# Splitting the load of V's first weight half in the head, and joining two late loads of the down weights

## The chip, the cores and the metric

The kernel runs on one core of a Trainium2 chip. The metric is the device time of one execution in microseconds (us); lower is better. Three runs of the kernel before took 308.35 to 308.47 us, the median is 308.46 us.

The core has a matrix engine (TensorE, PE in the profile; its weight loads are listed apart as PEld), a vector engine (VectorE, DVE), a scalar engine (ScalarE, ACT), GpSimd (POOL) and a queue processor (SyncE, SP) that issues transfers between the device memory (DRAM) and the core's working memory. Sixteen transfer engines carry them out. Matrix products accumulate in banks of a memory of their own (PSUM).

## The reference

One input x of 2048 rows and 640 columns goes through two branches, and their results are added to x. Only A_x is used as x; B_x has the same shape and is ignored by the reference's sum.

```python
def _A_ref(x, wqkv, wo):            # H = 32 heads of Dh = 20, window W = 256
    qkv = (x @ wqkv).reshape(B, S, 3, H, Dh).transpose(2, 0, 3, 1, 4)
    q, k, v = qkv[0], qkv[1], qkv[2]
    scores = einsum("bhqd,bhkd->bhqk", q, k) * (Dh ** -0.5)
    mask = (idx[:, None] - idx[None, :] >= 0) & (idx[:, None] - idx[None, :] < W)
    p = softmax(where(mask, scores, -1e9))
    o = einsum("bhqk,bhkd->bhqd", p, v)
    return o.transpose(0, 2, 1, 3).reshape(B, S, D) @ wo

def _B_ref(x, w_gate, w_up, w_down):   # F = 1536
    h = sigmoid(x @ w_gate) * (x @ w_up)
    return h @ w_down

xn = layernorm(x)
return x + _A_ref(xn, wqkv, wo) + _B_ref(xn, w_gate, w_up, w_down)
```

All arrays are bfloat16.

## The kernel before

**Tiling.** The 2048 rows are four chunks (c = 0 to 3) of 512 rows, each of four row blocks of 128 (s = 0 to 3). The 640 columns of x are five contraction blocks of 128 (DC = 5, index d), the 1536 hidden columns twelve blocks (FC = 12, index f). The query, key and value weights are one tile `wqkv` of 128 x 5 x 1920; V's part is its last 640 columns, handled as two halves of 320 (HALF). `wg`, `wu` and `wd` hold the gate, up and down weights, `wo` the output weights.

**The order of instructions is the order of the program text.** Nothing is rescheduled: every engine and every queue works through its own instructions in the order in which the code issues them, and an instruction waits until the results and transfers that it needs are there. SP issues nearly all loads and stores, one after the other, so that an issue that waits holds up those behind it.

**The head** (lines 141 to 163, then 671 to 729). SP first issues three row blocks of x (s = 0, 1, 3; `load_rows`), then V's first half with `load_v(0)` (one transfer, all five contraction blocks), then row block 2, V's second half with `load_v(1)`, the q and k weights (`load_wqkv`), and the first halves of block 0 of `wg` and `wu` (lines 162 and 163). The rest of `wg` and `wu` comes later, when other steps have passed; the second half of block 0 of `wu` is issued at line 409, between the first loads of the spread q and k.

TensorE starts with ten dummy products (`warm`, line 202). VectorE and ScalarE normalise the row blocks in the order 0, 1, 3, 2; TensorE transposes each normalised block (`turn_pieces`, tile `pt`; five transposes), and the transposed pieces are copied to `xnT`, contraction blocks 0 to 2 in one copy and 3 to 4 in another. In TensorE's order come: the transposes of row block 0, three dummy products, the transposes of row block 1, V's first half of row blocks 0 and 1 (`v00`, `v10`, five products each, lines 692 and 697), the transposes of row block 3, `v01`, `v30`, `v11`, the transposes of row block 2, and the remaining V products. `project_v` (line 317) runs over d = 0 to 4 and takes `wqkv[:, d, ...]` as the moving operand. Then the q and k projections of chunk 0 follow (`proj_block`, tile `pqk`), whose results go through `st` tiles to DRAM (`sq`, `sk`) and come back spread over the partitions (`spread`, tiles `qT` and `kT`).

**The steady part.** `fill` is a list of pieces of TensorE work (gate and up products `gu...`, projections `qk...` and `v...`, output `out...`), pulled between the steps of the attention so that TensorE always has something to do. Some pieces only issue transfers. Among them, line 743 issues the blocks 0 to 7 of the down weights in three transfers, and the piece "wd" (line 750) the blocks 8 to 11 in four, one block each, behind the q and k work of chunk 1 and ahead of V of chunk 1; the piece "wo" (line 752) then loads the output weights with four transfers, and `g_out` (line 485) loads rows of x and uses `wd` in `down` (line 452). In `down`, f runs from 0 to 11, so blocks 8 to 11 are needed last.

Of the kernel before, what the change touches and what calls it, by code (L numbers as in the profile page):

```python
# [15 lines left out]
DC = D // P  # L16
FC = F // P
# [7 lines left out]
HALF = 320  # L25
# [44 lines left out]
def kernel(  # L70
# [11 lines left out]
    nc = tc.nc  # L82
# [37 lines left out]
    wqkv = const.tile([P, DC, 3 * D], BF16, name="wqkv")  # L120
    wqkv_r = A_wqkv.rearrange("(c p) n -> p c n", p=P)
    wg = [const.tile([P, DC, FS], BF16, name=f"wg{k}") for k in range(F // FS)]
    wu = [const.tile([P, DC, FS], BF16, name=f"wu{k}") for k in range(F // FS)]
    wd = const.tile([P, FC, D], BF16, name="wd")
# [9 lines left out]
    def load_rows(s, queue):  # L134
        queue.dma_start(out=xc[0][:, s, :], in_=xr[:, s, :])  # L135

    def load_v(hf):
        a = 2 * D + hf * HALF
        nc.sync.dma_start(out=wqkv[:, :, a:a + HALF], in_=wqkv_r[:, :, a:a + HALF])

    load_rows(0, nc.sync)
    load_rows(1, nc.sync)
    load_rows(3, nc.sync)
    load_v(0)
    load_rows(2, nc.sync)
    load_v(1)
    load_wqkv(0)
    load_wqkv(1)
# [246 lines left out]
    def g_qk(c, behind={}):  # L395
        for w in "qk":
            for m in range(DC):
                proj_block(w, c, m)
                behind.get((w, m), lambda: None)()
                yield 5 * MM  # L400
        if c:
            spread("q", c, 0, 2)
            spread("k", c, 0, 2)
        else:
            for r in range(2):
                spread("q", c, r, r + 1)
                spread("k", c, r, r + 1)
                if r == 0:
                    load_gu(wu, B_w_up, 0, FS // 2)

    def g_v(c):
        for s in range(SBC):
            new_v(c, s)
            for b in range(2):
                both_v(c, s, b, nc.scalar.copy if b else nc.vector.tensor_copy)
            if s == 1 and c > 1:
                spread_rest(c)
            yield 10 * 136
# [210 lines left out]
    def mix(a, b, first, every=1, rest=True):  # L629

        for k, cost in enumerate(a):
            yield cost
            if k >= first and (k - first) % every == 0:
                yield next(b, 0)
        if rest:
            yield from b
# [94 lines left out]
    fill = Fill()  # L731
# [3 lines left out]
    def later(load, *args):  # L735
        load(*args)
        yield 0
# [9 lines left out]
    fill.add("gu0a", mix(g_gu(0, 0, 6), first, 0), 6 * GU)  # L747
    fill.add("gu0b", mix(g_gu(0, 6, 9), beside, 0), 3 * GU)
    fill.add("qk1", g_qk(1, behind1), 50 * MM)
    fill.add("wd", later(load_wd, ((8, 9), (9, 10), (10, 11), (11, FC))), 0)  # L750
    fill.add("v1", mix(g_v(1), norms2, 2, 1, False), 40 * 136)
    fill.add("wo", later(load_wo), 0)
    fill.add("gu0c", mix(g_gu(0, 9, 12), norms2, 0, 1, False), 3 * GU)
# [112 lines left out]
```

## Time and profile before

| What | us |
|---|---|
| median of three runs | 308.46 |
| the profiled execution | 308.37 |
| its span (first to last instruction) | 306.6 |
| TensorE busy in the span | 302.8 |
| VectorE busy | 192.1 |
| ScalarE busy | 193.1 |
| GpSimd busy | 83.4 |

The granted TensorE clock is full in the whole span. The second part of the page cuts the span into 40 slices; two of its lines show how the transfers are spread. "DMA" is the busy share of the sixteen transfer engines in tenths, "GB/s" what they moved:

```profile
DMA  7998889879029522721052022550000210000301
GB/s 212 348 277 259 282 253 324 227 237 224 9 82 275 149 86 94 227 69 71 18 128 87 25 76 88 175 183 0 3 2 5 68 40 24 2 2 3 88 21 64
```

The transfers are dense in the first quarter of the span, where all weights come in, and thin after it. A slice is 7.7 us long, so the whole head lies in the first two.

In a chain or timeline a line reads: start, duration, engine, line of the code or tile, and how often. In the view of waits it reads: who waited, `<-`, for whom, total time, number of times, longest time. In the view of transfers: destination, `<-`, source, the issuing queue, how often, size, and the time from issue to landing.

### The profile page before, as it was taken

How to read it: one execution, taken by the hardware profiler on the slowest of the kernel's cores; microseconds unless marked ns; L12 is line 12 of the kernel's file. 1: busy time of each engine (PE TensorE's matmuls, PEld its weight loads, DVE VectorE, ACT ScalarE, POOL GpSimd, SP SyncE). 2: the span in 40 equal slices, each digit the busy share in tenths (PEclk: the TensorE clock that was granted, in tenths of full speed). 3: DMA queues.
4: the chain of work that ended last, by engine and by line, in shares of the span. 5: the costliest groups of instructions: out<-in, count | busy, mean ns of one | idle time of the engine just before them, and what ended most of it. 6: DMA issues, size and time to landing. Idle time of an engine off the chain costs nothing.

```text
span 306.6 us, 10171 instructions
## 1 busy us (share of the span) xinstructions
PE 302.8 (99%) x4434; PEld 165.5 (54%) x4434; DVE 192.1 (63%) x391; ACT 193.1 (63%) x183; POOL 83.4 (27%) x189
## 2 busy tenths in 40 slices
PE   8999999999999999999999999999999999999996
PEld 3654444564556654644556644644446665444774
DVE  5778899298984489487643666364483627465523
ACT  6923785977775458867656557768765466778000
POOL 5021234635314123512213132341314132221100
PEclk9999999999999999999999999999999999999999
DMA  7998889879029522721052022550000210000301
GB/s 212 348 277 259 282 253 324 227 237 224 9 82 275 149 86 94 227 69 71 18 128 87 25 76 88 175 183 0 3 2 5 68 40 24 2 2 3 88 21 64
DMA packets 35788, 36.86 MB, mean 120 GB/s; under 512 B 2976, under 2 KB 35488, under 8 KB 35744
## 3 DMA queue, kind: packets, MB, share of 16 engines
q1 hardware_dynamic: 34336, 33.84, 37.0%
q0 software_dynamic: 544, 1.61, 1.7%
q10 hardware_dynamic: 864, 0.77, 0.9%
q8 instruction: 34, 0.56, 0.8%
q14 instruction: 10, 0.08, 0.1%
HBM read 25.59 MB, written 11.44 MB: 121 GB/s over the span
## 4 chain that ended last, share of the span: by engine, by line
PE 97%; DMA 1%; ACT 0%; DVE 0%; SPq 0%; issue 0%
PE pg L431 18%; PE y L454 18%; PE pu L440 17%; PE pqk L283 15%; PE ps L517 9%; PE y L461 7%; PE acc L550 6%; PE pv L341 6%; PE pv L321 1%; DMA xc<-in_A_x_dram 1%; PE pt L236 0%; PE pvh L321 0%; ACT turn L657 0%; PE pwarm L200 0%; DVE turn L230 0%; SPq L135 0%
## 5 line engine op out<-in xcount | busy, mean ns | idle before, releaser
L523 ACT ACTIVATE pT<-ps 128x2048 bf16<-128x2048 f32 x75 | 140.8, 1877 | 55.0 <-PE ps L517 32.5
L506 POOL TENSOR_SCALAR_AFFINE_SELECT pT<-pT 64x256 bf16<-64x256 bf16 (+1 forms) x126 | 67.1, 532 | 179.6 <-ACT pT L523 121.6
L431 PE MATMUL pg<-xnT,wg 128*128 128x512 bf16 x240 | 59.9, 380 | 0.0
L440 PE MATMUL pu<-xnT,wu 128*128 128x512 bf16 x240 | 59.8, 380 | 0.0
L454 PE MATMUL y<-wd,h 128*128 128x320 bf16 (+2 forms) x396 | 56.8, 295 | 0.0
L444 DVE SCALAR_TENSOR_TENSOR h<-th,pu 128x512 bf16<-128x512 f32 x48 | 32.8, 683 | 35.0 <-ACT th L434 19.4
L454 PEld LDWEIGHTS <-h 128*128 128x128 bf16 x396 | 36.8, 98 | 15.9 <-issue 2.3
L534 DVE TENSOR_TENSOR pT<-pT,keep 128x512 bf16<-128x512 bf16 (+2 forms) x81 | 35.8, 449 | 15.0 <-ACT pT L523 14.2
L283 PE MATMUL pqk<-xnT,wqkv 128*128 128x512 bf16 x185 | 43.7, 380 | 0.0
L434 ACT ACTIVATE th<-pg 128x512 f32<-128x512 f32 x48 | 28.6, 595 | 20.2 <-PE pg L431 19.9
L440 PEld LDWEIGHTS <-wu 128*128 128x128 bf16 x240 | 22.2, 98 | 27.3 <-issue 2.2
L431 PEld LDWEIGHTS <-wg 128*128 128x128 bf16 x240 | 21.7, 98 | 26.4 <-issue 2.9
L517 PE MATMUL ps<-qT,kT 20*64 20x320 bf16 (+4 forms) x1440 | 32.0, 260 | 0.0
L561 DVE STREAM_TRANSPOSE t<-acc 128x512 f32<-128x512 f32 x32 | 21.0, 694 | 17.1 <-PE acc L550 17.1
L465 DVE SCALAR_TENSOR_TENSOR rows<-y,rows 128x320 bf16<-128x320 f32 x30 | 14.2, 488 | 25.3 <-PE y L461 20.4
L283 PEld LDWEIGHTS <-wqkv 128*128 128x128 bf16 x185 | 18.5, 103 | 19.7 <-issue 0.8
L517 PEld LDWEIGHTS <-kT 20*64 20x64 bf16 x1440 | 13.5, 103 | 27.4 <-issue 27.4
L461 PE MATMUL y<-wo,oc 128*128 128x320 bf16 (+2 forms) x165 | 24.2, 295 | 0.0
L550 PE MATMUL acc<-pT,v 64*32 64x320 bf16 (+4 forms) x1440 | 20.0, 253 | 0.0
L461 PEld LDWEIGHTS <-oc 128*128 128x128 bf16 x165 | 15.5, 98 | 6.7 <-issue 1.0
L550 PEld LDWEIGHTS <-v 64*32 64x32 bf16 x1440 | 17.0, 92 | 3.4 <-issue 0.9
L341 PE MATMUL pv<-wqkv,xnT 128*64 128x320 bf16 x240 | 17.4, 300 | 0.0
(65 smaller groups left out, 190.4 us busy)
## 6 DMA issues: line engine op xcount, KB each, us to landing
qT<-sq SPq DMA_DIRECT2D x16, 256.0 KB, 4.3
kT<-sk SPq DMA_DIRECT2D x16, 256.0 KB, 4.6
xc<-in_A_x_dram SPq DMA_DIRECT2D x16, 160.0 KB, 4.3
sq<-st SPq DMA_DIRECT2D x20, 128.0 KB, 3.4
sk<-st SPq DMA_DIRECT2D x20, 128.0 KB, 3.1
out_dram<-rows SPq DMA_DIRECT2D x15, 160.0 KB, 1.8
wg<-in_B_w_gate_dram SPq DMA_DIRECT2D x4, 480.0 KB, 7.9
wu<-in_B_w_up_dram SPq DMA_DIRECT2D x4, 480.0 KB, 7.6
```

The lines of the kernel that those rows point to most:

```text
L283: nc.tensor.matmul(ps, lhsT=wt[:, m, :], rhs=xnT[c][:, :, d, :], start=(d == 0), stop=(d == DC - 1))
L341: nc.tensor.matmul(ps[hf * U:(hf + 1) * U, 0:HALF], lhsT=xnT[c][:, s, d, rows], rhs=wqkv[:, d, 2 * D + hf * HALF:2 * D + (hf + 1) * HALF], ...
L431: nc.tensor.matmul(pg, lhsT=part(wg, d, f), rhs=xnT[c][:, :, d, :], start=(d == 0), stop=(d == DC - 1))
L440: nc.tensor.matmul(pu, lhsT=part(wu, d, f), rhs=xnT[c][:, :, d, :], start=(d == 0), stop=(d == DC - 1))
L444: nc.vector.scalar_tensor_tensor(out=h, in0=th, scalar=1.0, in1=pu, op0=ADD, op1=MULT)
L454: nc.tensor.matmul(y[:, 0:cut[1] - cut[0]], lhsT=ht[c, f][:, s * P:(s + 1) * P], rhs=wd[:, f, cut[0]:cut[1]], start=(f == 0), stop=False)
L461: nc.tensor.matmul(y[:, 0:cut[1] - cut[0]], lhsT=oc[c, m][:, s * P:(s + 1) * P], rhs=wo[:, m, cut[0]:cut[1]], start=False, stop=(m == DC - 1))
L506: nc.gpsimd.affine_select(out=part, in_=part, pattern=pattern, compare_op=GE, fill=0.0, base=-1 if sign > 0 else 0, channel_multiplier=sign)
L517: nc.tensor.matmul(ps[side * U:(side + 1) * U, i, col * U:(col + n) * U], lhsT=qk["k", kc, half][32 * i:32 * i + DH, 2 * r + side, kb * U: ...
L523: nc.scalar.activation(out=pt[:, :, 0:used, :], in_=ps[:, :, 0:used * U], func=EXP, scale=SCALE)
L534: nc.vector.tensor_tensor(out=part, in0=part, in1=limit.to_broadcast([P, HG, n * U]), op=MIN)
L550: nc.tensor.matmul(accs[side][32 * i:32 * i + 32, q * U:(q + n) * U], lhsT=vt[sb][rows, b, at:at + 32], rhs=pt[rows, i, col:col + n, :], s ...
```

## The change

V's first half is loaded by two transfers, contraction blocks 0 to 2 and 3 to 4, in the place of one. The second of them stands ahead of row block 2 in SP's order. The late part of the down weights is loaded by three transfers in the place of four: blocks 8, 9, and 10 with 11. The number of transfers in the whole program stays the same. No product, copy or other instruction of an engine is changed.

```diff
-    def load_v(hf):
+    def load_v(hf, lo=0, hi=DC):
         a = 2 * D + hf * HALF
-        nc.sync.dma_start(out=wqkv[:, :, a:a + HALF], in_=wqkv_r[:, :, a:a + HALF])
+        nc.sync.dma_start(out=wqkv[:, lo:hi, a:a + HALF], in_=wqkv_r[:, lo:hi, a:a + HALF])
 
     load_rows(0, nc.sync)
     load_rows(1, nc.sync)
     load_rows(3, nc.sync)
-    load_v(0)
+    load_v(0, 0, 3)
+    load_v(0, 3, DC)
     load_rows(2, nc.sync)
     load_v(1)
     load_wqkv(0)
...
-    fill.add("wd", later(load_wd, ((8, 9), (9, 10), (10, 11), (11, FC))), 0)
+    fill.add("wd", later(load_wd, ((8, 9), (9, 10), (10, FC))), 0)
```

## The prediction

> **What bounds the kernel now.** I read the page first: busy shares and the chain that ended last.
>
> ```profile
> span 306.6 us, 10171 instructions
> PE 302.8 (99%) x4434; PEld 165.5 (54%) x4434; DVE 192.1 (63%) x391; ACT 193.1 (63%) x183; POOL 83.4 (27%) x189
> PE 97%; DMA 1%; ACT 0%; DVE 0%; SPq 0%; issue 0%
> ```
>
> TensorE (PE) makes up 97% of the chain, so a transfer counts only where TensorE stands still for it. Next, who TensorE's matmuls waited for; this is the view's whole answer for the run:
>
> ```profile
> PE pwarm L200 <- PEq L850: 0.8, 1, 0.8
> PE pt L236 <- DVE turn L230: 0.2, 1, 0.2
> ```
>
> No matmul waits for a transfer anywhere. Then the chain in order of time over the head, 3 to 14 us:
>
> ```profile
> 3.51 0.83 ACT turn L657 x2
> ...
> 6.44 0.45 PE pt L236 x5
> 6.89 1.36 PE pv L321 x10
> 8.25 0.30 PE pt L236 x5
> 8.54 1.36 PE pv L321 x10
> 9.90 0.68 PE pvh L321 x5
> ```
>
> The pieces join end to end: row block 1's transposes (`pt`), then the ten V matmuls (`pv`, first the five of `v00`) at 0.136 us each. The timeline has the first `pv` start at 6.73, one step after the fifth transpose began (6.44 + 5 x 0.058). Ahead of 6.44 the weight loads stood 0.53 us until VectorE's norm of row block 1 (L668): the head is set by row block 1, not by V's weights.
>
> The timeline of the SP queue gives the issues:
>
> ```profile
> 2.19 0.43 SPq L139 DMA_DIRECT2D wqkv<-in_A_wqkv_dram  x1
> 2.67 0.52 SPq L135 DMA_DIRECT2D xc<-in_A_x_dram  x1
> 3.23 0.43 SPq L139 DMA_DIRECT2D wqkv<-in_A_wqkv_dram  x1
> ```
>
> and the transfer view, asked one issue at a time, gives the time to landing. These are V's first half, issued at 2.19, and the second half of `wu`'s block 0, issued at 27.13:
>
> ```profile
> wqkv<-in_A_wqkv_dram SPq DMA_DIRECT2D x1, 400.0 KB, 4.3
> wu<-in_B_w_up_dram SPq DMA_DIRECT2D x1, 480.0 KB, 4.2
> ```
>
> So V's first half lands at 2.19 + 4.3 = 6.5, 0.24 us before its first use at 6.73. The `wu` piece lands at 27.13 + 4.2 = 31.33; TensorE needs it at 31.60 (`pu` of f = 3, whose columns begin at 384). That 0.27 us is the thinnest cover that I found behind the head.
>
> **The change, part by part.**
>
> *The wait that splits.* `v00`'s matmuls d = 0 to 2 now wait for the first piece, d = 3 and 4 for the second. The first is issued where the whole was (2.19) and carries 3/5 of the bytes. At best it lands earlier; at worst it keeps 4.3 us: 6.5 against 6.73, no stall and no gain, because row block 1's transposes stand ahead of it in TensorE's order. The second piece is issued one issue later. I take 0.48 us for that, the distance 2.67 - 2.19. With the whole 4.3 us kept it lands at 6.97, and d = 3 starts at 6.73 + 3 x 0.136 = 7.14. Cover left: 0.17 us. Behind the possibly waiting matmul stand all of TensorE's later matmuls; the value is 0 at both bounds. No row shows the cost of one more semaphore wait on a matmul. The nearest are the gaps marked issue, 0.02 to 0.04 us each in the head's chain; I take 0 and keep 0 to 0.04.
>
> *The issue added on SP.* Everything behind it moves 0.48 us later in issue: rows 2, V's second half, q and k weights, the first `wg` and `wu` pieces. Whether the landings move too depends on whether the 16 transfer engines run out of work. By the stage table they moved 51, 236, 325, 246, 159, 161, 244 GB/s in the half microseconds from 1.5 on, some 306 KB by 3.0 us. After the change the SP queue will have issued 491 KB of rows (three of 160 x 1024 bytes) plus 410 KB of V by 3.1 us: some 550 KB still pending, over 1.5 us of work at the later 350 GB/s. So I take 0 for the landings. The other end is the whole 0.48 us, with the same time to landing for each:
>
> - rows 2: 2.67 + 4.3 = 7.0 becomes 7.45. ScalarE takes it up at 7.26 (L657), so 0.19 late; its norm ends at 10.11, then 10.30, and TensorE transposes it at 10.42. Covered.
> - V's second half: 3.23 + 4.8 = 8.03 becomes 8.51; `v01` starts at 8.38. Stall 0.13.
> - q weights: 3.71 + 6.6 = 10.3; first used at 12.74. Covered by 2.4.
> - The `wu` piece at 31.33 hangs on the stream through a chain: the first q store lands late behind some 2 MB of loads, ScalarE's k copies wait for its `st` buffer until 21.94, the last k store follows, then `kT`, which SP waits for, and then the `wu` issue at 27.13. A delay of 0.48 would pass down it: 31.81 against 31.60, a stall of 0.21, which contains the 0.13 if that was already paid.
>
> So the sum over the head lies between 0 and +0.21 (0.25 with the wait's 0.04).
>
> *Transfers counted.* The extra transfer moves no extra bytes: pieces of 640 bytes in both. Its own time on the engines beyond bytes has no row here. From below it is 0; from above, the smallest issue-to-landing time in the head, 2.2 us (row block 1), if none of that ran beside other work. Row blocks 0, 1 and 3 land at 3.1, 3.5 and 4.6, though each took 2.2 to 2.9; most of that time therefore overlaps. The nearest row is the 0.4 us between the first two landings, about what 164 KB needs at 350 GB/s (0.47), so I take 0.
>
> The Trainium skill speaks against this edit: "DMA: Bandwidth & Descriptors", section Rules for kernel authors, says to coalesce small transfers into large ones, and its section on the anatomy of one DMA gives about 2.0 us of fixed cost each (a fit for transfers issued from GpSimd). [...]
>
> *The down weights.* Issues of 160 KB four times become 160, 160 and 320 KB:
>
> ```profile
> 66.80 1.90 SPq L172 DMA_DIRECT2D wd<-in_B_w_down_dram  x4
> 69.01 2.72 SPq L184 DMA_DIRECT2D wo<-wo_i  x4
> 72.13 1.11 SPq L471 DMA_DIRECT2D rows<-in_A_x_dram  x2
> 88.78 0.38 SPq L256 DMA_DIRECT2D turn<-turn  x1
> ```
>
> One issue goes, 1.90 / 4 = 0.48 us on SP; `wo` and `rows` may be issued that much sooner. TensorE's first down matmuls (`y`, L454) start at 81.81. The last piece, issued near 67.8, would land by 75.0 even with the 7.2 us that a 480 KB piece of `wd` took at most. `wo` (69 to 71.7, some 6.9 to landing) is used at 88.14. SP afterwards stands 15.2 us for VectorE's `turn` before 88.78, which takes up any shift. Value 0 both ways, covered by 6.8 us at the least.
>
> SP also waits for older transfers: it stood 0.4 us for a `wd` piece twice ahead of the `rows` loads. That looks like a wait for the transfer eight issues back. If so, one more transfer in the head makes the `wg` and `wu` issues wait for row blocks 1 and 3, landed by 4.6, before those issues (5.8 and later), and the count is level again after `wd`. Value 0.
>
> Sum: 0, with ends -0.06 (one transpose step, if V's landing was hidden in rounding) and +0.25. The profiled execution took 308.37 us: 306.6 of span and 1.77 around it. The median of the runs is 308.46, 0.09 above. I predict 308.45.
>
> **Rivals.**
>
> 1. *V's landing did set the start.* Earlier weights gain what TensorE lost to them. For it: 6.5 against 6.73 is thin. Against: `pt` and `pv` join without a gap, and before 6.44 VectorE was late. If row block 1 also landed sooner because less was queued behind it, the most would be ScalarE's idle time before it, 0.49 us: 307.97. A gain over 0.2% has no place that I can name, as TensorE never stands later.
> 2. *Slower: the late issue reaches the `wu` piece.* Place: `pu` of f = 3 at 31.60. It decides once the stream is more than 0.27 us later at the q stores. At 0.48 us it costs 0.21: 308.67. To pass 0.2% the delay must exceed 0.62 + 0.27 = 0.89 us, nearly two issues; for it only that engines moved just 160 GB/s from 3.5 to 4.5, a stretch that I can't explain and in which the added transfer lies.
> 3. *Slower: the extra transfer's fixed time stands in series.* Everything behind it lands 2.2 us later: V's second half at 10.2 against 8.38 stalls 1.85, and the `wu` piece (33.5 against then 33.45) hardly adds. 308.45 + 1.9 = 310.35. Against: the landings 0.4 us apart. With the skill's 2.0 us in its place this would be 0.2 us less.
> 4. *The split does nothing,* both pieces landing together at 6.5: 308.45, not to be told from the forecast by time.
>
> **How the numbers follow.** A measurement of this kernel tells about 0.2%, 0.62 us, from no change. No change (with rival 4): 0.55. Rival 1: 0.17; what I can price of it stays below 0.62 us, and 0.05 goes there; 0.12 is kept for a gain over the line by something of the head's transfers that the trace of before doesn't show. Rival 2: 0.20, of it 0.03 at its priced 0.21 us and 0.17 where the delay is more than I bounded. Rival 3: 0.08. So faster 0.12, within 0.55 + 0.05 + 0.03 = 0.63, slower 0.17 + 0.08 = 0.25. The likeliest case's own range is 308.2 to 308.7. The range from 307.9 to 309.2 takes in rival 1's bound and a stall of rival 2 up to 0.75 us, and leaves out rival 3 and the far ends.
>
> **What would show it.** In the changed profile: two `wqkv` issues of 240 and 160 KB from 2.19 on and rows 2 issued near 3.15; first `pv` still at 6.73 behind `pt` with no gap; `pvh` and `pqk` starts unmoved within 0.1; `pu` of f = 3 at 31.6. I am wrong if a matmul waits for `wqkv` or `wu`, if `pt` of row block 1 moves from 6.44, or if the steady stage after 45 us takes another length.

## The result: 0.3 to 0.4% slower

The changed kernel took 309.46 us (median of 8 runs, 308.87 to 310.15) against 308.47 us (8 runs, 308.35 to 308.93): ratio 1.0031, interval 1.0022 to 1.0041. Two repetitions in the later comparisons gave 1.0043 (1.0029 to 1.0057) and 1.0033 (1.0023 to 1.0043). The profiled execution took 309.37 us, its span is 307.6 us, 1.0 us over that of the kernel before.

The page of the changed kernel, span, busy shares and the chain by engine:

```profile
span 307.6 us, 10172 instructions
PE 303.1 (99%) x4434; PEld 165.6 (54%) x4434; DVE 192.2 (62%) x391; ACT 193.2 (63%) x183; POOL 83.2 (27%) x189
PE 95%; DMA 3%; SPq 1%; issue 0%; DVE 0%
```

A transfer now has 3% of the chain, and the queue processor 1%. Whom TensorE's matmuls waited for, the view's whole answer (who, `<-`, for whom: total us, times, longest; the first line is the start of the program and stood there before too):

```profile
PE pwarm L201 <- PEq L851: 0.8, 1, 0.8
PE pqk L284 <- DMA wqkv<-in_A_wqkv_dram: 0.6, 1, 0.6
PE pt L237 <- DVE turn L231: 0.2, 1, 0.2
```

and the chain in order of time from 3 to 15 us:

```profile
3.70 0.43 SPq L139
...
4.18 0.53 SPq L129
...
4.75 9.18 DMA wqkv<-in_A_wqkv_dram
...
13.97 1.06 PE pqk L284 x4
```

The loss is whole by 14 us. Matmul by matmul, the shift against the kernel before is 0.13 us at the first transposes, 0.21 at `v01` (8.60 against 8.38) and 0.98 at the second `pqk` (13.97 against 12.99); later it stays there. That second product of q waits for the transfer issued at 4.75: the **k** weights, not q's. The program has this wait in both kernels: the second weight load of q waits for the semaphore of the k transfer, though it reads q's columns alone. In the profile of before it left one line, in the view of the weight loads' waits:

```profile
PEld L283 <- DMA wqkv<-in_A_wqkv_dram: 0.3, 1, 0.3
```

The k weights landed there at 12.95, just as TensorE came to them. With the change they land at 13.93. The timelines of the weight loads have that place, first in the kernel before, then in the changed one (start, duration; in brackets how long the weight loads stood before it, and for whom):

```profile
12.99 1.67 PEld L283 LDWEIGHTS <-wqkv 128*128 128x128 bf16 x9 [0.27 <-DMA wqkv<-in_A_wqkv_dram]
```

```profile
13.97 0.59 PEld L284 LDWEIGHTS <-wqkv 128*128 128x128 bf16 x4 [1.04 <-DMA wqkv<-in_A_wqkv_dram]
```

How the transfers moved. Issues on SP after the change:

```profile
2.18 0.96 SPq L139 DMA_DIRECT2D wqkv<-in_A_wqkv_dram  x2
3.19 0.47 SPq L135 DMA_DIRECT2D xc<-in_A_x_dram  x1
3.70 0.43 SPq L139 DMA_DIRECT2D wqkv<-in_A_wqkv_dram  x1
```

The two pieces took 3.7 and 3.6 us to land (5.9 and 6.3), and row block 2 landed at 6.7: all **earlier** than before (6.5 and 7.0), although the last two were issued 0.5 us later. V's second half, issued at 3.70, landed at 8.6 against 8.0. What lies between is in the stage table. Its last two columns are the busy share of the transfer engines (above 1 where packets overlap) and GB/s; first the kernel before, then the changed one:

```profile
5.00:7.00 2.00, 1.75 (x16) 0.98 (x16) 1.84 (x7) 1.40 (x5) 0.00 (x0) 1.00 1.11 355
7.00:9.00 2.00, 2.00 (x20) 1.44 (x18) 1.92 (x8) 1.91 (x5) 0.00 (x0) 1.00 1.04 361
```

```profile
5.00:7.00 2.00, 1.77 (x16) 0.89 (x16) 1.84 (x6) 1.53 (x5) 0.00 (x0) 1.00 1.03 302
7.00:9.00 2.00, 2.00 (x19) 1.40 (x17) 1.92 (x8) 1.78 (x5) 0.00 (x0) 1.00 0.99 304
```

From 3 to 5 us the rate is higher by 20 GB/s, from 5 to 9 lower by 53 and 57. That is 180 KB less by 9 us ((53 + 57 - 20) x 2), or 0.48 us at the 376 GB/s that the kernel before moves from 9 to 11. So the stream came to be late by about one issue. These are single executions, but others go the same way: in these two rows the two further profiles with the head of the kernel before (`wd_only` and `before_own_k` below) have 329 to 361 GB/s, three with the split (`split_only`, `after_own_k`, `after_again`) 252 to 319.

### The profile page after: what moved, and what is told of

Its sections match the earlier page's. It is cut to its first block, busy times and chain, and to the rows that moved or that the text cites. A ratio compares the mean times of both kernels' runs of the same rounds, so it can differ in the third digit from the quotient of the medians.

```text
span 307.6 us, 10172 instructions
## 1 busy us (share of the span) xinstructions
PE 303.1 (99%) x4434; PEld 165.6 (54%) x4434; DVE 192.2 (62%) x391; ACT 193.2 (63%) x183; POOL 83.2 (27%) x189
## 4 chain that ended last, share of the span: by engine, by line
PE 95%; DMA 3%; SPq 1%; issue 0%; DVE 0%
PE pg L432 18%; PE y L455 18%; PE pu L441 17%; PE pqk L284 14%; PE ps L518 9%; PE y L462 7%; PE acc L551 6%; PE pv L342 6%; DMA wqkv<-in_A_wqkv_dram 3%; SPq L135 1%; SPq L139 0%; SPq L129 0%; DVE xc L466 0%
```

## The experiments

Theory A: the extra issue delays the k weights, and the wait for them is the whole loss; the down weights do nothing. B: the down weights cost something. C: the whole stream is late, and the next transfer stops TensorE if this one doesn't. Ratios are to the kernel before, run on the same chip, with a 95% interval.

**One part alone.** The changed kernel with the down weights as before:

```diff
-    fill.add("wd", later(load_wd, ((8, 9), (9, 10), (10, FC))), 0)
+    fill.add("wd", later(load_wd, ((8, 9), (9, 10), (10, 11), (11, FC))), 0)
```

> V's first half in two transfers, the down weights as before (160 KB four times). Theory A (the whole loss arises in the head, where the second q weight load waits for the k weights, and they land later behind one more issue): ratio 1.002 to 1.004 to the kernel before, and in the profile a wait of TensorE for wqkv of 0.5 us or more ahead of the second pqk. Theory B (the three late down pieces cost something, for example by later waits of SP): about 1.000.

and the kernel before with the three pieces:

> The down weights in three late transfers, V's first half in one. Theory A: 1.000 within 0.0007, no wait of TensorE for a transfer after 14 us. Theory B: 1.002 or more.

Measured: 1.0056 (1.0043 to 1.0070) and 1.0001 (0.9992 to 1.0010). The head's split makes all of the loss, the down weights nothing. (Why the split alone lies above all three measurements of the whole change, 1.0031 to 1.0043, is not explained.) But the stall of the first was elsewhere than expected, one wait earlier:

```profile
PE pv L322 <- DMA wqkv<-in_A_wqkv_dram: 0.7, 1, 0.7
```

V's second half (issued 3.70, 5.6 us to landing) came at 9.3; `v01` began 0.9 us late. With that, the k weights (13.7) came in time.

**The k weights apart.** `wqkv` is cut into a tile for q and V and one for k; the transfers stay.

```diff
+    wk = const.tile([P, DC, D], BF16, name="wk")
...
-    place = {(w, d): wqkv[:, d, base:base + D] for w, base in (("q", 0), ("k", D)) for d in range(DC)}
+    place = {(w, d): wk[:, d, :] if w == "k" else wqkv[:, d, 0:D] for w in "qk" for d in range(DC)}
```

> The changed kernel with the k weights in a tile of their own, so that q's products wait for the q weights alone; the transfers, their sizes and their order stay. Theory A (the wait for the k weights carries the loss): the stall ahead of the second pqk is gone, and about 0.2 us of the 1.0 us are left, which the profile of the change shows ahead of that place: ratio 0.9995 to 1.001. Theory C (the whole transfer stream is later, so that the next transfer stops TensorE as long, the q weights themselves or the second wu half before pu of f = 3): 1.002 or more, with TensorE waiting for wqkv, wg or wu elsewhere.

> The kernel before with the k weights in a tile of their own. The profile before shows 0.27 us of weight load idle and some 0.07 us of matmul idle at that place, so theory A: 0.9990 to 1.0000, 308.2 to 308.45 us, and a smaller spread over the runs than the 308.35 to 308.93 of the kernel before, as its slowest runs would be those in which the k weights land late. Theory C: the same time and the same spread.

Measured: 1.0037 (1.0025 to 1.0050) and 1.0003 (0.9994 to 1.0012), with a spread of 308.43 to 309.36. The needless wait is gone from the program, and the loss isn't. In the profile of the first:

```profile
PE pv L324 <- DMA wqkv<-in_A_wqkv_dram: 0.5, 1, 0.5
```

Theory A fell as to the single wait. C stood: `v01` waited and began 0.73 us late against before.

**Later issue or two pieces?** Theory D: SP's later issues are the cause; E: the two pieces are, whoever issues them. First, the second piece on ScalarE's queue (its first activation and the fill that it needs are moved up):

```diff
-    load_v(0, 3, DC)
+    load_v(0, 3, DC, nc.scalar)
```

> The second piece of V's first half is issued by ScalarE behind its first activation, which is moved up, so that SP issues row 2, V's second half and the q and k weights as early as in the kernel before; the same transfers, the same bytes. Theory D (the later issue on SP is the cause: V's second half is issued 0.48 us later, and the transfer engines run out of work ahead of it): V's second half lands at 8.0 to 8.3 us as before, ratio 0.9995 to 1.001. Theory E (the transfer in two pieces is the cause, whoever issues it, as each start of a transfer costs the engines): it lands at 8.5 or later, ratio 1.002 to 1.005.

Measured 1.0021 (1.0012 to 1.0030), and it decides for neither: the queue issued the piece at 0.94, ahead of row block 1, which ScalarE took up at 4.05 instead of 3.51. TensorE waited there and for no weight afterwards:

```profile
PE pt L237 <- DVE turn L231: 1.2, 1, 1.2
```

So it was held back by a fill of one element per partition on GpSimd, put behind GpSimd's first large fill, which the transfer has to wait for:

```diff
+    nc.gpsimd.memset(zero[:, 0:3, :], 0.0)
+    nc.gpsimd.memset(wqkv[:, 3, 2 * D:2 * D + 1], 0.0)
```

> V's second piece on ScalarE's queue, as in the run piece_on_act, where it was issued at 0.94 us, ahead of row block 1, and that block came 0.5 us late. Now it waits for GpSimd's first fill and one more small fill, so it is issued near 2.3 us. Theory D (the later issues on SP are the cause): row block 1 near 3.5 us, V's second half at 8.0 to 8.3, ratio 0.9995 to 1.001. Theory E (the two pieces themselves): V's second half late and 1.002 or more. Half way, 1.0010 to 1.0020: both have a part.

Measured 1.0010 (0.9999 to 1.0021). Beside it on the same chip the changed kernel, with `v01` at 9.26:

> The changed kernel once more, beside the three below on one chip: 1.002 to 1.005. It is what they are read against, since the ratios of different calls spread by 0.002.

Measured 1.0043 (1.0029 to 1.0057). Now the piece was issued at 2.29 and V's second half at 3.20. `v01` began at 8.63, straight behind the transposes; the first V product instead was 0.26 us late, as V's first piece landed only at 7.0 beside the other queue's transfer. With the same two pieces and SP on time, most of the loss is gone (the second piece is here also issued 0.37 us earlier than in the changed kernel).

The other way round, one piece and a later SP: a tiny load behind it (16 rows of 640 bytes).

```diff
+    load_v(0)
+    nc.sync.dma_start(out=spare[0:16, 0:HALF], in_=x2[0:16, 0:HALF])
```

> V's first half in one transfer as before, and behind it one more load on SP of 16 rows of 640 bytes of x into a buffer that nothing reads. Theory D: an issue more on SP at the same place, so the same loss as the change, ratio 1.002 to 1.005, V's second half issued at 3.70 and landing at 8.5 or later. Theory E: next to no bytes and V in one piece, ratio 0.9995 to 1.001.

and two of them:

> V's first half in one transfer and two tiny loads of 16 rows of 640 bytes behind it: V's second half is issued 0.96 us later than before. The run tiny_issue gave 1.0017. Theory D: the loss grows with the delay, 1.003 to 1.006. Theory E: next to nothing more than one tiny load, 1.001 to 1.002.

Measured 1.0017 (1.0008 to 1.0026) and 1.0048 (1.0032 to 1.0065). An issue that carries 10 KB costs, and a second one costs more. No run delays SP without a transfer, so the issue is not parted from the small transfer that it starts. For the first again, beside the changed kernel:

> V's first half in one transfer and one tiny load behind it, once more beside the changed kernel. If the later issue alone makes the loss, the same as the run after_third, within 0.0015. If the two pieces add to it, 1.001 to 1.0025 as before, clearly below.

> The changed kernel as the measure for the three below on the same chip: 1.003 to 1.0055.

Measured 1.0017 (1.0006 to 1.0027) and 1.0033 (1.0023 to 1.0043). By this pair the later issue makes about half of the loss. That the pieces themselves add the rest is likely but not settled: the two intervals overlap, and in `piece_on_act_later` the interval of what is left reaches no change.

In the stage row of 5 to 7 us, `tiny_two` (V in one piece, V's second half issued at 4.16) has the same dip, deeper:

```profile
5.00:7.00 2.00, 2.00 (x12) 1.09 (x12) 1.76 (x6) 1.36 (x6) 0.00 (x0) 1.00 0.94 232
```

That profiled execution, though, doesn't show the stall: V's second half landed at 8.10, hardly later than in the kernel before, and no matmul waited for a transfer. `v01` began 0.41 us late behind dummy products that ran slower, and the span of 307.7 isn't explained by `v01` alone. So the ratio of `tiny_two` stands without a profile that shows where its time went.

**Where an issue is free.** The q weights in two transfers, V's first half in one:

```diff
-    load_wqkv(0)
+    load_wqkv(0, 0, 3)
+    load_wqkv(0, 3, DC)
```

> V's first half in one transfer; the q weights in two instead, contraction blocks 0 to 2 and 3 to 4, so the extra issue stands behind V's second half. Theory D: V's second half lands as before (8.0 to 8.3); the engines have 1.6 MB queued by then, so the extra issue hides, and only the k weights may land a little later than 12.95: ratio 0.9995 to 1.0015. Theory E: 1.002 or more, since the q transfer has the extra start.

Measured 0.9999 (0.9989 to 1.0009). One more transfer and one more issue at no cost, a place behind V's second half. Its profiled execution was one of the longer ones (309.14 us): V's second half, issued at 3.23 as before, came late all the same, and `v01` started at 9.22. Landings vary from execution to execution; that the change shifts how often they stop TensorE is the likely reading, not shown, with one profile per run.

**Other orders.** The changed kernel with V's second half ahead of row block 2:

> The changed kernel with V's second half issued ahead of row block 2, at 3.19 us, where the kernel before has it at 3.23. Theory D: V's second half lands at 8.0 or earlier, and row block 2, now issued at 3.67, lands about 8; ScalarE takes it up some 0.7 us late, of which some 0.5 us are covered; the k weights are still an issue late: ratio 1.001 to 1.003. Theory E: 1.003 or more, with V's second half at 8.5 or later.

Measured 1.0034 (1.0021 to 1.0047). `v01` didn't wait; row block 1 came late (4.09) in that execution, and TensorE then waited for row block 2's norm. And the kernel before with row block 2 on ScalarE's queue:

> The kernel before with row block 2 issued on ScalarE's queue near 2.3 us, so SP issues V's second half, q and k one issue earlier, near 2.7, 3.2 and 3.7 us. Theory D taken the other way: the kernel before loses some of its slower executions to late landings, so 0.998 to 0.9995. Theory E: 1.000. Against both: two queues share the transfer engines, so row block 2 may land ahead of V's first half and hold it up, 1.001 or more.

Measured 1.0008 (1.0000 to 1.0017): no gain; the first V product waited 0.2 us for V's first half. No version beat the kernel before.

**Both waits away.** Theory G: the waits of `v01` and for the k weights carry the loss. In the last two, row block 0's product `v01` reads V's first half of the weights, so that nothing needs the second half before 9.9 us; the proper second half of V is left out for that row block, and the two serve for timing alone.

```diff
-    v01 = project_v(0, 0, 1)
+    v01 = project_v(0, 0, 0)
```

> The changed kernel, in which row block 0's product for V's second half reads V's first half of the weights instead (that part of V is wrong), so that the first wait for V's second half moves from 8.4 us to about 9.9. Theory G (the waits for V's second half at v01 and, behind it, for the k weights carry the loss): the first wait is gone, and what is left is the one for the k weights, which landed at 13.5 to 13.9 in the profiles of the changed kernel against 12.99: 1.001 to 1.003. Rival (row block 1's jitter or something behind the head): no less than the run after_third.

> The same with the k weights in a tile of their own, so that both waits are gone (the same part of V is wrong). Theory G: 0.9990 to 1.0010. Rival: 1.002 or more.

Measured 1.0044 (1.0031 to 1.0057) and 1.0033 (1.0021 to 1.0045). Theory G fell too, and C holds: with one wait removed, the next transfer stops TensorE. In `after_v01` the stall went to the k weights (`v01` began 0.44 us late in that profile as well, behind dummy products that ran slower, as in `tiny_two`):

```profile
PE pqk L284 <- DMA wqkv<-in_A_wqkv_dram: 0.8, 1, 0.8
```

With the k weights apart as well, the head up to the q products ran exactly as before (`pqk` at 12.74), and TensorE stopped at `pu` of f = 3, at 32.66 instead of 31.60 (0.29 us of this arose at the first `pg`, 23.89 instead of 23.60, which waited for ScalarE's copies). The kernel before issued that piece of `wu` at 27.13:

```profile
27.13 0.46 SPq L159 DMA_DIRECT2D wu<-in_B_w_up_dram  x1
```

The chain of waits from 20 to 34 us in `after_own_k_v01`:

```profile
19.42 4.69 DMA sq<-st
...
24.22 1.09 ACT st L292 x2
...
26.07 2.11 DMA sk<-st
...
28.72 3.89 DMA wu<-in_B_w_up_dram
...
32.66 1.25 PE pu L443 x5
```

A q store lands late, ScalarE's k copies wait for its buffer, the k store follows, then `kT`, and only then is the second half of `wu` issued, at 28.72 instead of 27.13. The same edit of `v01` was not run in the kernel before; the k weights' own tile costs nothing there (1.0003).

## Why the prediction was wrong

**The step that failed** is "the issue added on SP", where it took 0 for the landings and 0.21 us for the worst. It argued that 550 KB were pending at 3.1 us, over 1.5 us of work, so that an issue 0.48 us later would be hidden. It wasn't: the profile shows a lower rate from 5 to 9 us and the stream some 0.48 us behind. Even the upper bound was too small, as it kept the time to landing: V's second half took 4.9, 5.4 and 5.6 us in three profiles with the split against 4.8, so it landed 0.5 to 1.2 us later; q's weights landed 1.35 us later in the changed kernel (11.67 against 10.32) and k's 0.98. A transfer runs in sixteen parts, and TensorE waits for the last. By the time when fifteen of them were done, V's second half, q and k were 0.33, 0.47 and 0.43 us later in that profile, which the bound of 0.48 covers; the sixteenth part made up the rest.

**What was left out** is the k weights. The list of covers has q's at 2.4 us and passes over k's, whose line stood in the waits of the weight loads; its "No matmul waits for a transfer anywhere" rests on the matmuls' waits alone. A matmul that waits for `wqkv`, its own first sign of being wrong, then appeared. "The thinnest cover behind the head" was therefore not the 0.27 us ahead of `pu`: the k weights had next to none.

**Rival 2** named the right chain and the right place (`pu` of f = 3 at 31.60), and `after_own_k_v01` shows it link by link, with 1.06 us for a `wu` issue 1.59 us later. Its rule was right, its delay was not. In the changed kernel itself it is the third of three: `v01`, then k, then `wu`. Mostly whichever comes first takes the delay, and the others are then covered; in the profile of `tiny_again` two of them add up, 0.8 us at `v01` and 0.5 us at `pu`.

**Right:** the down weights cost nothing (1.0001), and SP's 0.8 us of waits for `wd` ahead of the `rows` loads are gone. The split brought nothing at the first V product, which still followed the transposes (6.86), though its weights landed 0.6 us sooner. **Rival 3**, a fixed time in series, is refuted in size: 1 us was lost, not 1.9, and `split_q` adds a transfer for nothing. The advice of the Trainium skill ("DMA: Bandwidth & Descriptors", Rules for kernel authors) to coalesce small transfers had the sign right here; the row there is about many small transfers, these are of 240 and 160 KB, and in `split_q` the same kind of split was free a place later.

**Open:** why the rate falls and one part comes so late. The stage rows don't show idle engines: the busy share falls only from 1.11 and 1.04 to 1.03 and 0.99, less than the rate does. One guess is that a transfer needs about 2 us before it flows, so that 1.5 us of pending work didn't cover it. In the changed kernel the dip does begin about 2 us after the issue of V's second half (3.70; 312 GB/s from 5.5 to 6 against 365), but in `tiny_two` it begins earlier behind its issue (4.16; 241 GB/s from 5.0 to 5.5 and 155 in the next half microsecond). No run isolated it.

## What to carry to other kernels

An issue put in front of others on one queue must be charged to every transfer behind it, with the spread of landings on top, until one is found whose cover is larger. List the covers of all of these, weight loads' waits included: several thin ones in a row act as one, and removing the first only shows the second. In this kernel one transfer more was free behind V's second half (0.9999) and cost 0.2 to 0.6% ahead of it (1.0017 to 1.0056); that the deeper queue behind it is the reason is likely, not shown.

## What the runs showed of the hardware

The trace records for each transfer when its sixteen parts complete. V's second half had its first part done at 7.07 and its last at 8.04 in the kernel before, at 7.09 and 8.55 in the changed one, and at 7.24 and 9.26 in `split_only`: the fastest part hardly moved, the slowest, which TensorE waits for, by up to 1.2 us.

Often it is one part alone. Of the k weights in the changed kernel fifteen parts were done by 13.01, the last at 13.93 (before: 12.58 and 12.95). Of V's second half it was 8.53 and 9.21 in `after_again`, 8.36 and 9.08 in `after_third`, and 8.47 and 9.18 in `split_q`; but 9.16 and 9.26 in `split_only`. In the three profiles with the head of the kernel before (`before`, `wd_only`, `before_own_k`) the two lie 0.02 to 0.14 us apart. The trace has single packets to go with it. Half of the load packets that start between 5 and 8 us take 0.03 us, and 95% at most 0.07. A few take 0.5 us or more: at most one in each of those three profiles, the longest 0.55 us, and one to eight in each of the seven with the split, the longest 1.47 us (in `after_v01`). What makes them slow, and whether the change makes more of them, no run shows.

The kernel before itself ranged over 308.18 to 309.63 us in 24 and 29 runs beside the experiments, more than its first three runs (308.35 to 308.47) let expect. Two queues issuing at the same time did not help: with the second piece on ScalarE's queue (2.29 us) V's first piece landed at 7.0 (4.8 us after its issue, against 3.7). That the two queues share the engines is the likely reason; no run parts it from others.
